# Forward convolution spread over more TensorE work: later transposes, eight residues for three more slices, and a drain one block later

## The chip, the cores and the metric

The kernel runs on one core of a Trainium2 chip. A core has TensorE (PE, matrix products into the accumulator memory PSUM), VectorE (DVE), ScalarE (ACT), GpSimd (POOL) and SyncE (SP), which share an on-chip memory (SBUF)[...]. The metric is the device time of one execution in microseconds (us). Before the change it is 1932.07 us, the median of three runs (1931.62 to 1939.0). The profile shown is of one execution with a span of 1928.7 us.

## The reference

The program computes a layer and its gradients. With S = 2048 rows, D = 1024 columns and F = 3584 hidden columns:

```
xn  = layernorm(q)                             # rows of 1024
ks  = causal 4-tap convolution of k over rows, one filter per column
kv  = ks * v
y   = causal convolution of kv with ssm_k over all 2048 rows (by FFT), per column
y   = y + kv * ssm_D
s   = xn * y
b   = ((xn @ w_gate) * (xn @ w_up)) @ w_down   # gate and up product, h, down product
out = q + s * silu(b)
outputs: out and the gradients to q, k, v, shift_k, ssm_k, ssm_D, w_gate, w_up, w_down
```

All inputs and outputs are bf16. The change touches the forward part alone: the layer norm, the gate and up product, the convolution y, and the beginning of the down product.

## The kernel before, in words

**Rows and slices.** The 2048 rows are 16 row blocks of 128. The F columns are 14 slabs of 256. The D columns of the convolution are eight slices of 128 (`ds`).

**Layer norm (`layer_norm`).** It works on chunks of rows: row blocks 0, 1, 2-3, 4-7, 8-11, 12-15. For each row block it normalises x on VectorE (for two of four blocks a part on ScalarE), turns the block with eight 128x128 transposes on TensorE into a PSUM tile `tr`, and copies that to `XNT`, alternately on ScalarE and VectorE. The norm of a chunk is recorded ahead of the products of the chunk before it.

**Gate and up product (`gu_unit`).** A unit is one slab by up to four row blocks. For each row block, eight matmuls of 512 columns go into `psg`, ScalarE copies the result to `gut`, and `tick()` is called. After a unit `multiply` makes h on VectorE (`hN`, 128x1024 in bf16, 60 such multiplies in all); five ticks later `turn` transposes it on TensorE and ScalarE copies it to `hT`, which is stored to `HTd`. `gut` is stored to `GUd`, h to `Hd`.

**Forward convolution (`conv_forward`).** It is a Python generator which records VectorE, ScalarE and TensorE instructions in small pieces and yields a weight for each. `tick` calls `pump`, which runs the generator until its summed weights reach the share of the total that the count of ticks gives; `NT` is the number of ticks that the total is spread over. So the convolution is interleaved with the products by this planned share[...]. For each slice, two spectra are made: matmuls with tables of sines and cosines into `psF`, ScalarE copies to `SP` (two buffers), sums on VectorE into `W`, then `KX` or `HX`. The spectra are multiplied (`product`), and the inverse begins with sums on VectorE and ends with matmuls into `psY` (`tail`), which ScalarE copies to `yf`, stored to `YFd`.

**Two forms of the inverse.** `inv_dft` with `inv_rows` folds the 16 residue segments with few VectorE sums and does 32 matmuls of 256 columns a slice. `inv8` with `inv8_rows` goes one level further on VectorE and does 16 matmuls. `INV8` lists the slices with the second form; before the change these are 2 and 5. `F_TOTAL` adds its weight.

**Down product (`bm_mm`, `bm_first`, the loop over `bp`).** Row block b of `h @ w_down` takes 28 times two matmuls of 512 columns into a PSUM tile `psbm`. Blocks 0 and 1 are done together (`bm_first`, with ticks of 0.74), in the two buffers of `ps_bm`. Then `drain()` records what is left of the convolution, the convolution's memory is released, and the gates of blocks 0 and 1 are recorded. The loop over `bp` from 1 to 7 does the blocks 2*bp and 2*bp+1. Block 2 is in a buffer of its own (`ps_bx`), block 3 uses the first buffer of `ps_bm` again, and so needs block 0's result copied away. The h columns of a pair come from `load_ht`; pairs from the second on alternate between two buffers, `mh0` and `mh1`.

**Gates (`gate`).** For a row block, four tiles are loaded by SyncE (`x_t`, `do_t`, `xn_t`, `yf_t`, two buffers each; `yf_t` reads what the convolution stored in `YFd`). ScalarE copies `psbm` to `bm` and makes two sigmoids, VectorE makes eleven products and sums of 128x1024 (the first are named `so`, `dgg`, `gg`), GpSimd stores four results (`dbm` goes to `DBMd`). After every four blocks a transposing load of `DBMd` is queued on SyncE.

The rest of the program is the backward part, whose code is unchanged.

Of the kernel before, what the change touches and what calls it, by code (L numbers as in the profile page):

```python
# [13 lines left out]
BF16 = mybir.dt.bfloat16  # L14
# [5 lines left out]
def build_kernel(  # L20
# [11 lines left out]
    nc = tc.nc  # L32
    P = 128
# [31 lines left out]
    def st(out, in_):  # L65
        ins = nc.gpsimd.dma_start(out=out, in_=in_)  # L66
        if PINQ[0]:
            tc.keep_in_program_order(ins)
        return ins
# [17 lines left out]
    def pool(name, bufs=1, side=None, space=None):  # L87
        kw = dict(name=name, bufs=bufs, reuse_waits="tile")
        if side:
            kw["side"] = side  # L90
        if space is not None:
            kw["space"] = space
        return tc.alloc_tile_pool(**kw)
# [455 lines left out]
            ld(x4[:, 0:n, :], xq[:, c, r0:r0 + n, :])  # L549

    tr_ln, act_copy = [None], [None]

    def layer_norm(b0, n, x4):
        def small(name, dt=F32):
            return lns.tile([P, 4], dt, name=name)[:, 0:n]
        mv = lns.tile([P, 4, 2], F32, name="mv")[:, 0:n, :]
        for i in range(n):
            bst = lns.tile([P, 2, 6], F32, name="bst")
            for hh in range(2):
                V.bn_stats(out=bst[:, hh, :], in_=x4[:, i, hh * 512:(hh + 1) * 512])  # L560
            V.bn_aggr(out=mv[:, i, :], in_=bst[:])
        var_b = small("var_b", BF16)
        V.tensor_copy(var_b, mv[:, :, 1])
        vpe = small("vpe", BF16)
        V.tensor_scalar(vpe, var_b, EPS, None, op0=ADD)
        r0_ = small("r0_")
        with tc.issue_after(act_copy[0].ins) if act_copy[0] is not None else nullcontext():
            root = nc.scalar.activation(r0_, vpe, ACT.Sqrt)
        mean_b = small("mean_b", BF16)
        V.tensor_copy(mean_b, mv[:, :, 0])  # L570
        rr0 = small("rr0")
        V.reciprocal(rr0, r0_)
        mean_f = small("mean_f")
        V.tensor_scalar(mean_f, mean_b, -1.0, None, op0=MUL)
        q0 = small("q0")
        tt(q0, vpe, rr0, MUL)
        r1 = small("r1")
        tt(r1, r0_, q0, ADD)
        sq_b = small("sq_b", BF16)
        V.tensor_scalar(sq_b, r1, 0.5, None, op0=MUL)  # L580
        V.reciprocal(RSTD[:, b0:b0 + n], sq_b)
        for i in range(n):
            b = b0 + i
            q, qi = divmod(b, 4)
            if n == 4 and i < 2:
                nc.scalar.activation(x4[:, i, :], x4[:, i, :], ACT.Identity, bias=mean_f[:, i:i + 1])
            else:
                V.tensor_scalar(x4[:, i, :], x4[:, i, :], mean_f[:, i:i + 1], None, op0=ADD)
            last = V.tensor_scalar(x4[:, i, :], x4[:, i, :], RSTD[:, b:b + 1], None, op0=MUL)
            if b < 2:  # L590
                for hh in range(2):
                    ps = ps_st.tile([P, 4, P], BF16, name="tr")
                    for dc in range(4):
                        d0 = (4 * hh + dc) * P
                        tr_ln[0] = nc.tensor.transpose(ps[:, dc, :], x4[:, i, d0:d0 + P], ident[:])
                    act_copy[0] = nc.scalar.copy(out=XNT[0][:, 4 * hh:4 * hh + 4, b * P:b * P + P], in_=ps[:])
                if b == 0:
                    with tc.issue_after(tr_ln[0].ins):
                        keep_busy(10)
                continue  # L600
            ps = ps_st.tile([P, DC, P], BF16, name="tr")
            for dc in range(DC):
                tr_ln[0] = nc.tensor.transpose(ps[:, dc, :], x4[:, i, dc * P:(dc + 1) * P], ident[:])
            if i % 2 == 0:
                act_copy[0] = nc.scalar.copy(out=XNT[q][:, :, qi * P:(qi + 1) * P], in_=ps[:])
            else:
                V.tensor_copy(XNT[q][:, :, qi * P:(qi + 1) * P], ps[:])
        c, r0 = divmod(b0, 8)
        return last, root, st(xnn[:, c, r0:r0 + n, :], x4[:, 0:n, :])

    nop = lambda: None
    nop1 = lambda c: None
# [6 lines left out]
    def flush(age=0):  # L619

        for e in later:
            e[0] += 1
        while later and later[0][0] >= age:
            later.pop(0)[1]()
# [5 lines left out]
    def gu_unit(sl, b0, n, w, tick):  # L630

        if n == 4:
            turn_of[0] += 1
            if turn_of[0] % 3 == 0 and sl < NSL - 2:
                gut = U[5][:, 2048:4096].rearrange("p (a i f) -> p a i f", a=2, i=4)
            else:
                gut = fg.tile([P, 2, 4, SLW], BF16, name="gut")
            hN = fg.tile([P, 2, 4, P], BF16, name="hN", bufs=3)
        else:
            gut = lnp.tile([P, 2, 2, SLW], BF16, name="gut_s", bufs=6)  # L640
            hN = lnp.tile([P, 2, 2, P], BF16, name="hN_s", bufs=6)
        for i in range(n):
            q, qi = divmod(b0 + i, 4)
            ps = ps_gu.tile([P, 512], F32, name="psg")
            for dc in range(DC):
                gu_mm[0] = nc.tensor.matmul(ps[:], XNT[q][:, dc, qi * P:(qi + 1) * P],  # L646
                                            w[:, dc].rearrange("p a f -> p (a f)"), start=(dc == 0), stop=(dc == DC - 1))
            nc.scalar.copy(out=gut[:, :, i], in_=ps[:].rearrange("p (a f) -> p a f", a=2))  # L648
            flush(5)
            hn[0]()  # L650
            hn[0] = nop
            tick()
        sta(GUd[sl, b0 // 8][:, :, b0 % 8:b0 % 8 + n], gut[:, :, 0:n])

        def multiply():
            with tc.issue_after(last.ins) if b0 + n <= 4 and chunk[0] <= 2 else nullcontext():
                by_half = lambda t: t.rearrange("p i (a f) -> p a i f", a=2)
                tt(hN[:, :, 0:n], by_half(gut[:, 0, 0:n]), by_half(gut[:, 1, 0:n]), MUL)
            st(Hd[sl][:, :, b0:b0 + n, :], hN[:, :, 0:n])
            defer(turn)  # L660
        hn[0] = multiply

        def store(hT):
            fr, so = sl % 12 * SLW, b0 % 8 * P
            ld(HTd[b0 // 8][sl // 12][fr:fr + SLW, so:so + n * P].rearrange("(a f) s -> f a s", f=P),
               hT[:, :, 0:n].rearrange("f a i s -> f a (i s)"))

        def turn():
            hT = fg.tile([P, 2, 4, P], BF16, name="hT") if chunk[0] > 5 else lnp.tile([P, 2, 4, P], BF16, name="hT_s", bufs=5)
            ps = ps_tr.tile([P, 2, 4, P], BF16, name="tr")  # L670
            for a in range(2):
                for i in range(n):
                    nc.tensor.transpose(ps[:, a, i, :], hN[:, a, i, :], ident[:])
            nc.scalar.copy(out=hT[:, :, 0:n], in_=ps[:, :, 0:n])
            store(hT)

    h_out = []
    EIGHT = ((0, 0), (0, 1), (7, 0), (7, 1))
    INV8 = (2, 5)
    SHIFT_W = 8 * 2.3  # L680

    conv_state = {"forward": True}
# [227 lines left out]
    ps_cv = pool("ps_cv", 2, space=PSUM)  # L910
    pump, drain = make_pump(conv, F_TOTAL)
    cnt = [-5]
    NT = 24 * 8.0 + 14

    def tick(by=1):
        cnt[0] += by
        if cnt[0] == -4:
            pump((SHIFT_W + 4.05) / F_TOTAL)
        if cnt[0] >= -2:
            pump((SHIFT_W + (F_TOTAL - SHIFT_W) * (cnt[0] + 5) / (NT + 2)) / F_TOTAL)  # L920

# [331 lines left out]
        ht1 = load_ht(1)  # L1253
    ht2 = load_ht(2)
    bm_first(range(4, NF))
    drain()
    PIN[0] = False
    mh.append(pool("mh1", 1, side="right"))
    mi = pool("mi", 2, side="right")
    mt = pool("mt", 1, side="right")  # L1260
    mo = pool("mo", 2, side="right")
    for i in range(2):
        gate(i, pss[i])
    for bp in range(1, 8):
        ht, ht_ld = load_ht(bp) if bp > 2 else (ht1, ht2)[bp - 1]
        if bp in (3, 5, 7):
            q = (bp - 3) // 2
            with tc.issue_after(ht_ld.ins):
                nc.sync.dma_start_transpose(out=DBMT[q], in_=DBMd[512 * q:512 * q + 512, :])
        if bp == 6:  # L1270
            with tc.issue_after(ht_ld.ins):
                wdt = load_wdt(0)
                gu_in(0)
        for i in range(2):
            ps = (ps_bx if (2 * bp + i) % 3 == 2 else ps_bm).tile([P, D], F32, name="psbm")
            for fc in range(NF):
                bm_mm(ps, ht, i, fc)
                if fc == 18:
                    flush()
            gate(2 * bp + i, ps)  # L1280
    for p_ in (ps_bx, ps_tr, ps_y, ps_bm, mo, mt, mi, mh[1], mh[0]):
        p_.release()
# [346 lines left out]
```

## Time and profile before

| | us |
|---|---|
| time, median of three runs | 1932.07 |
| span of the profiled execution | 1928.7 |
| PE busy | 1907.8 |
| VectorE busy | 1542.7 |
| ScalarE busy | 638.8 |
| PE waits on a row-block transpose for VectorE's normalised rows, four times | 2.4 |
| PE starts the block products of the down product | 519.62 |
| VectorE ends the forward convolution | 528.1 |
| last `psY` matmuls of the forward convolution start | 549.21 |

A line of the timeline gives the start and the length of a run of like instructions, the engine, the line of the code, the operation, the output and inputs by the program's names, the shapes, the count, and in brackets how long the engine was idle before it and what ended this. In the slices (40 of them, 48.2 us each) a digit is the busy share in tenths. An answer on waiting gives the engine that waited, what it waited for, the sum in us, how often, and the longest. PE's end times are modelled and overlap with the next start, so the starts are used to count PE's work.

### The profile page before, as it was taken

The numbers are of one execution on the slowest core, as the hardware profiler recorded it, in microseconds if no ns is written. First come the engines' busy times: TensorE is split into PE (matmuls) and PEld (weight loads), VectorE is DVE, ScalarE is ACT, GpSimd is POOL, SyncE is SP. The second block draws the span as 40 slices with busy tenths as digits, with TensorE's granted clock in tenths as the row PEclk, the third lists the DMA queues.
The fourth block names the chain that finished last, engine by engine and source line by source line (L and its number), as shares of the span: only waits on it lengthen the run. The fifth ranks groups of instructions, "written<-read, shape, count | busy, mean of one in ns | idle before, by whom it ended". The sixth has DMA issues, their size and how long they took to land.

```text
span 1928.7 us, 27377 instructions
## 1 busy us (share of the span) xinstructions
PE 1907.8 (99%) x10860; PEld 1032.3 (54%) x10994; DVE 1542.7 (80%) x1720; ACT 638.8 (33%) x942; POOL 328.7 (17%) x461
## 2 busy tenths in 40 slices
PE   8999999999999999999999999999999999999999
PEld 5555555555444457665666666664444444444444
DVE  9999999999937556888799999999996403488873
ACT  5854555556323233343222222222222102011122
POOL 4121211201112210000122131021111101011111
PEclk9999999999999999999999999999999999999999
DMA  8876866758879997666788788575787999799973
GB/s 294 267 243 229 256 216 219 248 185 290 294 227 310 285 313 260 208 203 218 250 247 257 250 244 264 199 273 178 222 255 173 157 209 214 167 188 188 192 207 117
DMA packets 451360, 444.43 MB, mean 230 GB/s; under 512 B 268800, under 2 KB 371612, under 8 KB 436768
## 3 DMA queue, kind: packets, MB, share of 16 engines
q1 hardware_dynamic: 394848, 243.36, 47.8%
q0 software_dynamic: 40064, 169.95, 27.5%
q10 hardware_dynamic: 16320, 29.36, 4.2%
q8 instruction: 86, 1.41, 0.3%
q14 instruction: 42, 0.34, 0.1%
HBM read 194.00 MB, written 185.64 MB: 197 GB/s over the span
## 4 chain that ended last, share of the span: by engine, by line
PE 84%; DVE 11%; issue 2%; ACT 1%; DMA 1%; SPq 0%; ACTq 0%; DVEq 0%
PE psb L1337 20%; PE psx L1467 20%; PE psb L1320 10%; PE psbm L967 10%; PE psb L1415 9%; PE psg L646 9%; DVE W L213 3%; DVE HX L213 2%; DVE KX L213 2%; PE psF L235 2%; DVE U L213 1%; DVE m L213 1%; PE psY L438 1%; DVE hN L213 1%; PE psY L1114 1%
## 5 line engine op out<-in xcount | busy, mean ns | idle before, releaser
L646 PE MATMUL psg<-wslab,U 128*128 128x512 bf16 x1735 | 400.5, 379 | 5.9 <-ACT gut L648 1.7
L1337 PE MATMUL psb<-U,U 128*128 128x512 bf16 x1792 | 397.1, 379 | 0.0
L1467 PE MATMUL psx<-U,dgut 128*128 128x512 bf16 x1505 | 331.1, 379 | 1.6
L1467 PEld LDWEIGHTS <-dgut 128*128 128x128 bf16 x1792 | 175.3, 98 | 211.5
L1337 PEld LDWEIGHTS <-U 128*128 128x128 bf16 x1792 | 175.2, 98 | 198.0
L646 PEld LDWEIGHTS <-U 128*128 128x128 bf16 x1792 | 172.5, 98 | 188.9 <-issue 3.5
L1320 PE MATMUL psb<-wdt,U 128*128 128x256 bf16 x1792 | 205.6, 273 | 0.0
L1320 PEld LDWEIGHTS <-U 128*128 128x128 bf16 x1792 | 175.2, 98 | 29.3
L1415 PE MATMUL psb<-U,U 128*128 128x512 bf16 x797 | 175.9, 380 | 0.9
L1342 ACT CAST wb<-psb 128x512 bf16<-128x512 f32 x112 | 65.5, 585 | 315.5 <-PE psb L1337 307.7
L213 DVE TENSOR_TENSOR W<-W 128x1024 f32<-128x1024 f32 (+1 forms) x168 | 165.4, 1001 | 3.6
L967 PE MATMUL psbm<-U,ht 128*128 128x512 bf16 x658 | 145.0, 379 | 0.7
L1415 PEld LDWEIGHTS <-U 128*128 128x128 bf16 x896 | 87.4, 98 | 104.6
L648 ACT CAST gut<-psg 128x512 bf16<-128x512 f32 x156 | 91.0, 587 | 129.4 <-PE psg L646 121.1
L1499 ACT ACTIVATE dx_t<-dxn 128x1024 bf16<-128x1024 f32 x15 | 15.9, 1057 | 324.8 <-DVE dxn L213 320.9
L967 PEld LDWEIGHTS <-ht 128*128 128x128 bf16 x672 | 65.6, 98 | 78.6
L213 DVE TENSOR_TENSOR U<-U,dht 128x2048 bf16<-128x2048 bf16 x56 | 68.3, 1221 | 45.9 <-ACT dht L1322 45.8
L1322 ACT CAST dht<-psb 128x512 bf16<-128x512 f32 x112 | 65.6, 586 | 116.4 <-PE psb L1320 116.4
L1166 DVE SCALAR_TENSOR_TENSOR dkp<-dkT,kT 128x1024 bf16<-128x1024 bf16 (+2 forms) x64 | 78.3, 1224 | 30.7 <-DMA dkT<-DKSHd 28.9
L213 DVE TENSOR_TENSOR dxn<-psx,dxna_t 128x1024 f32<-128x1024 f32 x15 | 18.3, 1222 | 87.9 <-PE psx L1467 83.9
L66 POOL DMA_DIRECT2D Hd<-hN x54 | 36.9, 684 | 263.3 <-DVE hN L213 261.0
L1446 ACT CAST wbs<-psb 128x512 bf16<-128x512 f32 x51 | 29.8, 585 | 145.1 <-PE psb L1415 131.2
(256 smaller groups left out, 2464.5 us busy)
## 6 DMA issues: line engine op xcount, KB each, us to landing
U<-GUd SPq DMA_DIRECT2D x28, 1024.0 KB, 7.6
DGd<-U SPq DMA_DIRECT2D x28, 1024.0 KB, 5.8
GUd<-gut ACTq DMA_DIRECT2D x39, 512.0 KB, 6.3
out_dram<-wb SPq DMA_DIRECT2D x112, 128.0 KB, 4.2
U<-Hd SPq DMA_DIRECT2D x14, 1024.0 KB, 6.5
Hd<-hN POOLq DMA_DIRECT2D x54, 256.0 KB, 5.0
HTd<-hT SPq DMA_DIRECT2D x52, 256.0 KB, 3.9
ht<-HTd SPq DMA_DIRECT2D x6, 1536.0 KB, 13.2
```

The lines of the kernel that those rows point to most:

```text
L213: pinned(V.tensor_tensor(o, a, b, op))
L235: mm = nc.tensor.matmul(ps[:, k].rearrange("p (c d) -> p c d", c=2), T[:, r, k, :], xr[:, r], start=(n == 0), stop=(n == len(rs) - 1 and ( ...
L646: gu_mm[0] = nc.tensor.matmul(ps[:], XNT[q][:, dc, qi * P:(qi + 1) * P], w[:, dc].rearrange("p a f -> p (a f)"), start=(dc == 0), stop=(dc ...
L648: nc.scalar.copy(out=gut[:, :, i], in_=ps[:].rearrange("p (a f) -> p a f", a=2))
L967: mm = nc.tensor.matmul(ps[:, dh * 512:(dh + 1) * 512], ht(fc)[:, i * P:(i + 1) * P], WD[fc // 4][:, fc % 4, dh * 512:(dh + 1) * 512], sta ...
L1166: ins = V.scalar_tensor_tensor(prod[:].rearrange("p r d -> p (r d)")[:, lo:H], dkT[:, 0, lo:H], 1.0, kT[:, 0, 13 + m + lo:13 + m + H], op0 ...
L1320: nc.tensor.matmul(ps[:, x * SLW:(x + 1) * SLW], DBMT[2 * hf + g][:, dc, (b % 4) * P:(b % 4 + 1) * P], wdt[:, dc, :], start=(dc == 0), sto ...
L1322: nc.scalar.copy(out=dht[:, 2 * e:2 * e + 2].rearrange("p b f -> p (b f)"), in_=ps[:])
L1337: nc.tensor.matmul(ps[:], XN[b // 4][:, b % 4, dc * P:(dc + 1) * P], dgus[b // 8][:, :, b % 8], start=(b == 0), stop=(b == NB - 1))
L1342: nc.scalar.copy(out=wb[:, dc % 2].rearrange("p a f -> p (a f)"), in_=ps[:])
L1415: nc.tensor.matmul(ps, h[:, f, b, :], DBM[b // 4][:, b % 4, dh * 512:(dh + 1) * 512], start=(b == 0), stop=(b == NB - 1))
L1467: nc.tensor.matmul(ps[:, dh * 512:(dh + 1) * 512], t[n][:, f, i * P:(i + 1) * P], WGU[n][:, f, dh * 512:(dh + 1) * 512], start=(n == 0 and ...
```

## The change

There are three edits to the forward part. They are meant to fill TensorE's waits in the beginning, to take matmuls off it, and to give the convolution a longer stretch of products to lie beside.

1. The transposes of row blocks 8 to 15 are not recorded in `layer_norm`. They are kept in `turn_rows`, and `turn_late()` records them after the first row block of the next gate and up unit.
2. Slices 1, 4 and 6 use `inv8` too.
3. The convolution is spread over four more ticks (`NT`), 14 ticks of 0.37 are added in block 2 of the down product, and the drain, the release of memory, the new pools and the gates of blocks 0 and 1 come behind block 2's matmuls.

```diff
+    turn_rows = []
...
+            if b0 >= 8:
+                turn_rows.append((x4[:, i, :], q, qi))
+                continue
             ps = ps_st.tile([P, DC, P], BF16, name="tr")
...
+    def turn_late():
+        for i, (x, q, qi) in enumerate(turn_rows):
+            ps = ps_st.tile([P, DC, P], BF16, name="tr")
+            for dc in range(DC):
+                tr_ln[0] = nc.tensor.transpose(ps[:, dc, :], x[:, dc * P:(dc + 1) * P], ident[:])
+            if i % 2 == 0:
+                act_copy[0] = nc.scalar.copy(out=XNT[q][:, :, qi * P:(qi + 1) * P], in_=ps[:])
+            else:
+                V.tensor_copy(XNT[q][:, :, qi * P:(qi + 1) * P], ps[:])
+        turn_rows.clear()
...
             flush(5)
+            if i == 0:
+                turn_late()
             hn[0]()
...
-    INV8 = (2, 5)
+    INV8 = (1, 2, 4, 5, 6)
...
-    NT = 24 * 8.0 + 14
+    NT = 24 * 8.0 + 18
...
     bm_first(range(4, NF))
-    drain()
-    PIN[0] = False
-    mh.append(pool("mh1", 1, side="right"))
-    mi = pool("mi", 2, side="right")
-    mt = pool("mt", 1, side="right")
-    mo = pool("mo", 2, side="right")
-    for i in range(2):
-        gate(i, pss[i])
     for bp in range(1, 8):
...
                 if fc == 18:
                     flush()
+                if 2 * bp + i == 2 and fc % 2 == 1:
+                    tick(0.37)
+            if 2 * bp + i == 2:
+                drain()
+                PIN[0] = False
+                mh.append(pool("mh1", 1, side="right"))
+                mi = pool("mi", 2, side="right")
+                mt = pool("mt", 1, side="right")
+                mo = pool("mo", 2, side="right")
+                for j in range(2):
+                    gate(j, pss[j])
             gate(2 * bp + i, ps)
```

## The prediction

> **What bounds the kernel now.** I read the page's slices first, then the busy table of three stretches, then who waits for whom, then single lines of the timeline around each edit.
>
> ```profile
> PE   8999999999999999999999999999999999999999
> DVE  9999999999937556888799999999996403488873
> ```
> ```profile
> 64.00:520.00 456.00, 448.74 (x2767) 252.65 (x2817) 447.11 (x405) 259.24 (x366) 76.42 (x109) 1.00 0.72 241
> 520.00:560.00 40.00, 39.72 (x208) 20.07 (x212) 9.60 (x9) 9.98 (x12) 1.83 (x2) 1.00 0.62 180
> 560.00:722.00 162.00, 161.22 (x769) 75.50 (x783) 104.03 (x165) 47.39 (x47) 37.98 (x60) 1.00 1.04 307
> ```
> The columns of the second fence are the stretch, its length, then PE, PEld, DVE, ACT and POOL busy, clock, DMA share and GB/s. PE looks like the bound everywhere. But in 64 to 520 us, the gate and up product with the forward convolution, VectorE is as full as PE (447 of 456 us). It rests after 528 us, and from 560 us the DMA engines are full (1.04).
>
> Which of two full engines sets the pace is told by waits. From the answers on waiting (whole program, then 64 to 560 us):
>
> ```profile
> ACT SP L257 <- DVE W L213: 4.2, 6, 1.4
> PE psF L235 <- ACT SP L257: 1.4, 5, 0.3
> DVE hN L213 <- ACT U L648: 4.3, 1, 4.3
> ```
> ```profile
> 427.87 1.93 ACT L257 COPY SP<-psF 128x1024 f32<-128x1024 f32 x2 [0.43 <-DVE W L213]
> ```
> ```profile
> 428.93 1.95 PE L235 MATMUL psF<-hx,TF 128*128 128x256 bf16 x16 [0.34 <-ACT SP L257]
> ```
> PE waits for ScalarE's spectrum copy, which waits for VectorE to have read the older copy. The waits are short, but they come back in slice after slice: in six of the eight slices the first copies of the second transform start 0.1 to 0.6 us after VectorE's read. VectorE itself waits three times: 4.28 us at 135.41, 0.43 at 496.11, 0.61 at 520.44; its other gaps add to 4.1 us in 105 pieces. So VectorE leads this stage, and PE keeps up by a small margin.
>
> [...] the 128x2048 f32 `W<-KX` takes 2,292 ns. So f32 operations of 512 columns, which the edit adds, can't be cheap: the trace has them at 686 ns. [...] the trace has 49 matmuls in 10.74 us, 216 ns, and I use that. [...] waits on PE are up to 0.16 us longer than printed (379 ns shown, 216 ns spacing). [...]
>
> **Part 1, late transposes.** Rows 8 to 15: the same 64 transposes and 8 evictions, behind eight matmuls instead of ahead of them. They remove two PE waits, 0.71 us at 37.32 and 0.64 at 48.26, 1.4 to 1.7 us with the hidden part. In 20 to 60 us VectorE is busy 39.1 of 40 us, and the order of the new kernel has the same VectorE work ahead of every h multiply up to 88 us. I take 0 for the end (bounds 0 and -1.7).
>
> **Part 2, eight residues in slices 1, 4, 6.** PE: 16 fewer 128x256 matmuls a slice; eight take 0.87 us (543.14 to 544.01), so 1.74 us a slice, 5.2 us in all. VectorE: `inv8` has the same two 2.29 us reads and, for four 1.22 us operations, four others of the same size, plus ten of 512 columns (four HX sums, two W, four scaled sums). Two such take 1.29 us, overlapped about 0.64 each: 6.4 us a slice, 19.2 us in all. VectorE leads, so this counts, except what fits in its rest or moves past the stage.
>
> **Part 3, convolution into the third block.** With the weaker ticks (NT 18) the last multiply (the 60th `hN`) has more convolution behind it. In the order before there remain HX, W, HX (2.36+2.29+2.36 = 7.0 us). In the new order also KX, m, two KX, W, HX, W, HX: 1.22+1.22+2.36+2.29+2.36+2.29+2.36 = 14.1 us. So 7.1 of the 19.2 us leave the stage and 12.1 stay. The order also puts 11.4 us more VectorE work ahead of the multiply at 135.41, which closes its 4.28 us hole; a slower VectorE doesn't meet the 0.43 and 0.61. The last multiply starts at 520.44+12.1-4.28-1.04 = 527.2, ends at 527.9, and its transposes follow at 527.95. Before:
>
> ```profile
> 524.78 0.61 PE L673 MATMUL tr<-ident,hN 128*128 128x128 bf16 x8
> 543.14 1.04 PE L449 MATMUL psY<-HX,TI 128*128 128x256 bf16 x8
> 549.21 1.04 PE L449 MATMUL psY<-HX,TI 128*128 128x256 bf16 x8
> 550.09 22.61 PE L967 MATMUL psbm<-U,U 128*128 128x512 bf16 x102
> ```
> At 524.78, same place in PE's order: **+3.2 us**, PE's 5.2 us spent in waiting. If all 4.1 us of small gaps went too, -0.9; if the hole stays open, +7.5.
>
> VectorE's tail then ends at about 527.9+14 = 542; the first `psY` of slice 7, 144 block matmuls after the block start instead of 104, comes at about 555. No wait there.
>
> **What the drain's move queues up.** In the new order four block matmuls (0.86 us) stand between the last `psY` and block 3, whose first matmul waits for ScalarE's `bm` of block 0. That came at 550.77 to 551.78, 2.57 us after the last `psY` started (549.21). PE gets there after 0.87+0.86 = 1.73 us: **+0.9 us**. Block 2 used to hide this.
>
> The gates of blocks 0 to 2 begin 44 matmuls later in PE's order, 9.5 us, 8.6 relative to PE after that wait. Their chain was not held by PE: the last YFd store (551.2, 6.6 us to land), `yf_t`, then gates 0 to 4 back to back with two DMA waits. Behind them in SyncE's queue stands the h load of the fifth block pair, which block 8 needs:
>
> ```profile
> 593.24 5.16 SPq L1269 DMA_TRANSPOSE U<-DBMd  x1
> 598.49 0.68 SPq L61 DMA_DIRECT2D do_t<-in_grad_out_dram  x1
> 601.18 0.60 SPq L61 DMA_DIRECT2D ht<-HTd  x1
> ```
> ```profile
> DMA to landing us min/median/max: 15.5/15.5/15.5
> ```
> ```profile
> 621.12 1.01 ACT L1198 CAST bm<-psbm 128x1024 bf16<-128x1024 f32 x1 [9.04 <-PE psbm L967]
> ```
> The second fence is of the load at 601.18 alone: landed 616.7. The DBMd transpose ahead of it starts when gate 3's store has landed (593.17). Block 8 starts at 620.9, as block 7's copy at 621.12 shows: a margin of 4.2 us. Shifted by 8.6, the load is 4.4 us late: **+4.4 us**, from 0 (with less traffic such a load takes 10 us, the median) to 7 (still more beside it). Later loads of this kind are issued at PE's release, with 14 us in hand.
>
> **Sum.** 3.2+0.9+4.4 = +8.5: 1932.1+8.5 = 1940.6 us. After block 8 the order is unchanged and PE hardly waits, so nothing gives it back.
>
> **Rivals.**
> - PE is the true bound. -5.2-1.6+0.9 = -5.9: 1926.2 us, faster. For it: PE 99%, printed waits tiny. Against: the copies tied to VectorE in six slices.
> - VectorE sets the pace, but the load arrives in time since its traffic thins out: +3.2+0.9 = +4.1, 1936.2 us. For it: other such loads take 10 us; against: the same transpose and gate loads stand around it.
> - VectorE loses more: the hole doesn't close (+4.3) and the load is 6 to 7 us late: about +15, 1947 us. For it: the DMA share of 1.04. Against: the new order has work ready for the hole.
>
> **How the numbers follow.** Forecast 0.45, PE bound 0.12, load in time 0.28, loses more 0.15. Leaving out PE bound and the upper half of the last, the range runs from 1930 (all gaps closed, load in time, some PE gain) to 1947. 0.5% is 9.7 us: slower means over 1941.7. That takes the last rival (0.15) and some 0.4 of the forecast (0.18): 0.33. Faster needs under 1922.4, which no case gives: 0.04. The rest, 0.63, is within.
>
> **What would show it.** Step 2 right: 19 us more VectorE work before the gates, with no gap at 135 us. Step 3: the last h transposes near 528 us, and new PE waits on `hN` or `SP` between 430 and 528. Then a wait of PE on `bm` of about 0.9 us at block 3, and one on `ht<-HTd` at block 8 of 2 to 6 us. Wrong if block products start before 517 us (PE was the bound), if the h load lands before block 7 ends, or if a wait appears after 720 us.

## The result and the profile after

The changed kernel takes 1944.14 us, the median of four runs (1942.38 to 1945.96), beside 1931.84 us for the kernel before (median of four). The ratio is 1.0055, with a 95% interval of 1.003 to 1.008: it is slower, and the ratio lies just over the half per cent that was to tell it from no change, though its interval reaches to both sides of that. The forecast of 1940.6 us was 3.5 us too low; the range of 1930 to 1947 holds the time. All runs of this case are in the same, fast state, and the ratios here and below are formed from all of them and not from two medians, so a ratio can differ from that of the medians. The profiled execution has a span of 1942.3 us, 13.6 us over the one before.

The page's slices after, for the two engines shown before:

```profile
PE   9999999999999999999999999999999999999999
DVE  9999999999938654888899899999997403487884
```

The two pictures are nearly the same: the slices don't show where 13.6 us went. The busy table of the three stretches does a little more (columns as in the prediction):

```profile
64.00:520.00 456.00, 441.67 (x2702) 247.01 (x2751) 451.12 (x424) 256.29 (x363) 74.89 (x108) 1.00 0.70 231
520.00:560.00 40.00, 36.97 (x184) 17.35 (x186) 22.25 (x18) 4.47 (x6) 1.68 (x3) 1.00 0.79 248
560.00:722.00 162.00, 159.11 (x750) 73.91 (x764) 98.13 (x156) 50.52 (x51) 36.57 (x57) 1.00 1.02 285
```

VectorE is busy 451 of 456 us in the first stretch (447 before) while PE's work there fell from 448.7 to 441.7. In the second PE lost 2.75 us of its 39.7, in the third 2.1 us. The answer on PE's waits names all the places:

```profile
PE psF L235 <- ACT SP L257: 8.4, 4, 3.1
PE tr L1237 <- DVE dbm L213: 2.9, 1, 2.9
PE psbm L984 <- DMA U<-in_B_w_down_dram: 2.5, 1, 2.5
PE psg L661 <- ACT gut L663: 2.1, 2, 1.9
PE psbm L984 <- DMA ht<-HTd: 1.4, 1, 1.4
...
PE tr L619 <- DVE U L590: 0.9, 2, 0.7
...
PE psbm L984 <- ACT bm L1215: 0.7, 1, 0.7
```

The wait on `SP` was 1.4 us before; the waits on `dbm`, on the `w_down` tile (`WD[6]`), on `ht` and on `bm` did not exist. The timeline of PE puts them in time, and the last transposes of h beside them:

```profile
528.35 0.62 PE L690 MATMUL tr<-ident,hN 128*128 128x128 bf16 x8 [0.32 <-DVE hN L213]
547.66 10.48 PE L984 MATMUL psbm<-U,U 128*128 128x512 bf16 x47 [2.50 <-DMA U<-in_B_w_down_dram]
567.75 12.25 PE L984 MATMUL psbm<-U,U 128*128 128x512 bf16 x55 [0.73 <-ACT bm L1215]
629.72 2.55 PE L984 MATMUL psbm<-U,ht 128*128 128x512 bf16 x11 [1.37 <-DMA ht<-HTd]
726.49 0.62 PE L1237 MATMUL tr<-ident,dbm 128*128 128x128 bf16 x8 [2.90 <-DVE dbm L213]
726.95 5.74 PE L984 MATMUL psbm<-U,ht 128*128 128x512 bf16 x17
```

The last two lines had no wait and full speed before:

```profile
714.58 0.61 PE L1220 MATMUL tr<-ident,dbm 128*128 128x128 bf16 x8
715.03 4.05 PE L967 MATMUL psbm<-U,ht 128*128 128x512 bf16 x17
```

How late PE stands at the same instruction of both traces turns these waits into a sum. The first block product starts at 522.89 us, 3.27 later than before. By ScalarE's copy of each block's result (`bm`), blocks 6 and 7 stand at +7.31, blocks 8 to 14 at +8.85 (one copy at +9.13), and the end of block 15 at +13.61; from there to the end nothing changes. So the 13.6 us are

| step | us | of it |
|---|---|---|
| gate and up stage | 3.27 | waits on `SP`, 8.4 in all (1.4 before); one has a halved clock behind it |
| blocks 0 to 5 | 4.04 | `WD[6]` 2.5, `bm` 0.73, each with 0.16 of hidden part (the prediction's 379 ns against 216), 0.5 of small ones |
| block 8 | 1.54 | `ht` 1.37 and the hidden part |
| block 15 | 4.76 | `dbm` 2.90 and the hidden part, and 1.7 of a halved clock |

The halved clock is seen in the last line of each of the two fences above: the same 17 recorded matmuls take 5.74 us where they took 4.05 before. The busy table of three short stretches shows the granted clock (third number from the end):

```profile
204.80:208.20 3.40, 3.20 (x16) 2.28 (x16) 3.40 (x4) 2.07 (x3) 0.00 (x0) 0.50 0.00 0
318.30:321.70 3.40, 2.83 (x21) 2.04 (x21) 3.40 (x4) 3.04 (x4) 0.00 (x0) 1.00 0.00 0
727.10:730.50 3.40, 3.40 (x10) 1.21 (x8) 1.96 (x3) 1.01 (x1) 0.71 (x2) 0.50 1.00 400
```

Beside PE waits of 3.12 us (up to 205.00) and 2.90 us (up to 726.49) it runs at 0.50 for 3.41 us, from 204.82 and from 727.06; after one of 2.69 us (up to 318.87) it stays at 1.00.

### The profile page after: what moved, and what is told of

It is laid out like the page before. It is cut to its first block, busy times and chain, and to the rows that moved or that the text cites. A ratio compares the mean times of both kernels' runs of the same rounds, so it can differ in the third digit from the quotient of the medians.

```text
span 1942.3 us, 27309 instructions
## 1 busy us (share of the span) xinstructions
PE 1907.1 (98%) x10813; PEld 1028.7 (53%) x10946; DVE 1561.6 (80%) x1750; ACT 638.2 (33%) x942; POOL 328.7 (17%) x461
## 4 chain that ended last, share of the span: by engine, by line
PE 62%; issue 0%; ACT 0%; DVE 0%; ACTq 0%
PE psb L1357 20%; PE psx L1487 20%; PE psb L1340 10%; PE psb L1435 9%; PE psY L1131 1%; PE psY L438 1%; PE psx L1435 1%; PE psF L235 1%; PE psbm L984 0%; PE psY L1435 0%; ACT B L295 0%; DVE dbm L213 0%; PE tr L1237 0%; ACT wbs L1582 0%; ACT wb L1362 0%
## 5 line engine op out<-in xcount | busy, mean ns | idle before, releaser
L213 DVE TENSOR_TENSOR W<-W 128x1024 f32<-128x1024 f32 (+1 forms) x186 | 184.0, 1005 | 3.9
L1466 ACT CAST wbs<-psb 128x512 bf16<-128x512 f32 x51 | 29.8, 585 | 145.3 <-PE psb L1435 134.4
```

The lines of the kernel that those rows point to most:

```text
L213: pinned(V.tensor_tensor(o, a, b, op))
```

## Experiments

Runs 1 to 3 take the change apart and run 4 goes the other way; all four begin with the kernel before. "First" is the start of the first block product, "span" that of the profiled execution, both as us over the kernel before; the ratio is to the runs of before on the same chip.

| run | kernel | median, us | ratio (95%) | first | span |
|---|---|---|---|---|---|
| 1 | late transposes alone | 1931.24 | 1.0001 (0.9992 to 1.0009) | -0.1 | -0.1 |
| 2 | five slices alone | 1943.32 | 1.0064 (1.005 to 1.0078) | +11.8 | +11.8 |
| 3 | moved drain alone | 1949.55 | 1.0099 (1.0082 to 1.0115) | -0.65 | +19.1 |
| 4 | before with no slice of eight residues | 1930.71 | 0.9995 (0.9987 to 1.0004) | +0.4 | +0.4 |
| 5 | changed, turns a block later | 1943.81 | 1.006 (1.0047 to 1.0072) | +3.9 | +12.4 |
| 6 | run 3, turns a block later | 1940.46 | 1.0053 (1.0033 to 1.0073) | +0.2 | +5.2 |
| 7 | changed, plain `DBMd` loads | 1939.58 | 1.0039 (1.0026 to 1.0052) | +2.9 | +8.1 |
| 8 | mix of three slices | 1954.6 | 1.0106 (1.0071 to 1.0142) | +3.75 | +14.9 |
| 9 | changed, `DBMd` loads later | 1963.92 | 1.0174 (1.015 to 1.0199) | +3.8 | +46.1 |
| 10 | run 8, third load later | 1955.16 | 1.0113 (1.0087 to 1.014) | +3.0 | +22.1 |
| 11 | before with three slices | 1933.07 | 1.0009 (1.0001 to 1.0017) | +5.6 | +5.6 |
| 12 | before with one slice | 1930.41 | 0.9992 (0.9986 to 0.9998) | -0.3 | -0.3 |

A profile is one execution, and not always one near the median. Those of runs 6 and 8 (1935.69 and 1945.37 us) lie 5 and 9 us below their medians; that of run 9 (1976.61 us) is the slowest of six, 13 us above.

**Run 1: part 1 alone.** The edit is the first part of the diff, on the kernel before.

> Part 1 alone on the kernel before. VectorE leads the stage: 0 (between -0.5 and +0.3 us), and only one of the two early PE waits (0.71 at 37.3, 0.64 at 48.3) goes, as in the changed kernel, where 0.71 and 0.17 stayed. PE is the bound: the removed wait shows at the end, -0.6 to -1.6 us.

The ratio is 1.0001: nothing. In the trace, as in that of the changed kernel, the wait of 0.71 us near 37.5 is still there, now of the late transposes themselves (`tr L619` in the waits above), and the one of 0.64 became 0.17. So the edit removed half a microsecond of PE's waits in a stretch where VectorE is full, and it doesn't show at the end.

**Run 2: part 2 alone.**

```diff
-    INV8 = (2, 5)
+    INV8 = (1, 2, 4, 5, 6)
```

> Part 2 alone: three more slices with eight residues, the drain at its old place. PE 5.2 us less work, VectorE 19 us more. VectorE leads: nothing moves behind the last hN, so the last hN and the first block products come 8 to 14 us later than before (hole of 4.28 us partly closed), and most of it stays to the end: +6 to +14 us. PE is the bound: about -5 us.

PE has 5 us less to do, and the kernel is 12.2 us slower: PE isn't the bound of this stage. All of it stands at the first block product (+11.8), and nothing is added later. The stage's row of the busy table, then PE's waits from 64 to 560 us, then a line of VectorE's timeline, all of run 2:

```profile
64.00:520.00 456.00, 436.68 (x2655) 243.84 (x2705) 451.64 (x424) 254.50 (x357) 75.45 (x107) 0.99 0.69 229
```
```profile
PE psF L235 <- ACT SP L257: 12.6, 5, 4.3
PE psF L235 <- DVE kv L213: 1.7, 1, 1.7
PE tr L673 <- DVE hN L213: 1.6, 1, 1.6
```
```profile
535.08 0.69 DVE L213 TENSOR_TENSOR hN<-gut 128x1024 bf16<-128x1024 bf16 x1
```

VectorE has no gap over 0.25 us from 60 to 540 us. The last line is the last h multiply. The prediction's own working, without the 7.1 us that part 3 moves behind it, puts it at 520.44 + 19.2 - 4.28 - 1.04 = 534.3 us; it started at 535.08. None of the later waits appear here: the `w_down` tile landed at 548.37 us, but PE, 11.8 us late itself, hadn't come to it by then.

**Run 3: part 3 alone.** `NT`, the ticks in block 2, and the drain, pools and gates behind block 2, with `INV8 = (2, 5)`.

> Part 3 alone with the old two slices of eight residues: convolution thinner ahead of the last hN. VectorE leads: block products start 2 to 6 us earlier than before (PE cannot gain more than its own waits), but the costs behind stay as in the changed kernel: WD load late 2.7, bm of block 0 0.9, h load at block 8 1.5, and 4.8 at block 15 (2.9 us wait with 1.7 us of halved clock), so in all +4 to +10 us. If those late waits come from VectorE's extra work instead of the moved drain and gates: they are absent and the time is -1 to -5 us. PE is the bound: +1.

This is the costliest part: +18.5 us, more than the whole change, and more than any branch of the expectation allowed. The waits on `dbm`, `ht` and `bm` are there with the two old slices, so VectorE's extra work isn't what makes them. The stage is 0.65 us shorter, where 2 to 6 had been expected, so everything is lost in the blocks. PE's waits of the whole program, the longest first:

```profile
PE tr L1220 <- DVE dbm L213: 12.2, 2, 8.2
PE psbm L967 <- DMA ht<-HTd: 2.5, 1, 2.5
```

The two waits on `dbm` are 8.19 us in block 13 and 4.00 in block 15, and 10.2 us of half clock go with them. Of these 2.8 lie within the first wait (the half clock runs from 698.02 to 704.84, the wait ends at 700.80), so 7.4 us at half speed cost 3.7. 12.2 + 3.7 + 2.5 (`ht`) + 0.7 (`bm`), with 0.16 of hidden part each, is 19.8, and -0.65 leads to +19.1. The 5.1 us in the expectation of run 6 counts the 2.8 too. SyncE's queue shows what the gates waited for. In this view the length is how long SyncE was held by the issue:

```profile
698.73 0.46 SPq L61 DMA_DIRECT2D x_t<-in_A_q_dram  x1
699.30 16.53 SPq L1261 DMA_TRANSPOSE U<-DBMd  x1
715.94 0.54 SPq L61 DMA_DIRECT2D do_t<-in_grad_out_dram  x1
716.92 0.33 SPq L61 DMA_DIRECT2D xn_t<-XNd  x1
717.35 0.40 SPq L61 DMA_DIRECT2D yf_t<-YFd  x1
```

The third transposing load of `DBMd` held the queue for 16.5 us and landed 24.0 us after its start, and the gate's four loads behind it landed from 724.8 to 726.8. In the trace of the kernel before this load took 15.2 us, but that is the longest of the six traces with the drain at its old place: they run from 6.3 us (run 11) to 15.2, and none has a wait on `dbm`.

**Run 4: the other direction.** `INV8 = ()` in the kernel before.

> Kernel before with no slice of eight residues: PE +3.5 us of matmuls, VectorE -12.8 us. VectorE leads: PE's waits of the stage vanish, the added matmuls lie in them, -2 to +1 us. PE is the bound: +3.5 us.

-0.4 us, so neither a bound on PE (+3.5) nor one on VectorE (which has 12.8 us less, by the prices of part 2) is seen. PE's waits on `SP` fall from 1.4 to 0.7 us, and PE is busy 452.2 of 456 us in the stage (448.7 before), so the added matmuls fill its small gaps. At two slices the two engines are in balance: work added to VectorE costs, work taken off it brings nothing, since PE is right behind.

**Runs 5 and 6: is it the wait in block 15?** `turn`, the transposes of a gate's `dbm` on PE, one row block later; run 5 in the changed kernel, run 6 in that of run 3.

```diff
                 if fc == 18:
-                    flush()
+                    flush(2)
```

> The changed kernel with the turns of gates 12 to 14 recorded one row block later (flush of age 2 in the loop). If the wait of 2.90 us at 726.49 and the halved clock behind it (1.7 us) cost what the trace shows: -4.8 us against the changed kernel, +8.8 against the kernel before, about 1940.6. If the gates' transfers are late anyway and PE only waits for them further on: 0 against the changed kernel.

> The moved drain alone (two slices of eight residues, as the run before with the drain alone), with the turns of gates 12 to 14 one row block later. If the 8.19 and 4.00 us of PE's waits and the 5.1 us of halved clock were its cost: +19.1 - 17.3 = about +2 us against the kernel before, from 0.7 (bm) + 2.5 (h load) - 0.65 (earlier block products). If late transfers hold PE further on: still +10 or more.

Run 5: the wait and its halved clock are gone from the trace, and the time isn't: 1943.81 us, as before the edit. PE's waits from 520 us on are now

```profile
PE psbm L984 <- DMA ht<-HTd: 2.8, 1, 2.8
PE psbm L984 <- DMA U<-in_B_w_down_dram: 2.3, 1, 2.3
PE psbm L984 <- ACT bm L1215: 0.7, 1, 0.7
```

with the clock halved behind the 2.84 us on `ht` (the 31 matmuls recorded there take 8.77 us, 283 ns each beside the prediction's 216): PE loses 4.7 us at block 8 instead of 1.5. Also, the third transposing load took 8.2 us from issue to landing here and 22.1 in the changed kernel's trace. SyncE's issue of it, in run 5 and then in the changed kernel:

```profile
695.66 5.05 SPq L1278 DMA_TRANSPOSE U<-DBMd  x1
```
```profile
694.75 12.27 SPq L1278 DMA_TRANSPOSE U<-DBMd  x1
```

The edit moves transposes on PE that come after the issue (from 698.4 us on in the changed kernel), which hardly explains that. And this shorter load, not the edit, took the wait away: gate 14's `dbm` was ready at 725.16, before PE reached the place in block 15 where the unedited order turns it (726.56). It rather seems that the length of such a load changes from one execution to the next, as the spread of the runs suggests (1939.11 to 1947.75 us in run 5), and a trace holds one of them. The 4.76 us of block 15 are right for the execution profiled; that the median has them is not shown. Run 6's trace has no wait after 630 us and stands at +5.2, where +2 was expected; about half of the difference is a halved clock (1.7 us) behind its `ht` wait of 2.3 us (mean clock 0.96 from 600 to 640 us). Here too the `dbm` of gates 12 and 14 were ready before PE came to their old places in blocks 13 and 15 (693.37 against about 694.8, one block ahead of 706.85, and 717.99 against 719.38), so the trace doesn't test the edit either. The eleven runs spread from 1934.99 to 1954.36 us, and their median is +8.9, 9.1 us under run 3's, with intervals that don't meet. That speaks for the `dbm` waits having carried a large share of run 3's cost, but not all of it; no trace shows it.

**Run 7: plain loads in place of the transposing ones.** The edit leaves out the turning of `DBMd`, so two of the weight gradients aren't those of the reference.

```diff
-                nc.sync.dma_start_transpose(out=DBMT[q], in_=DBMd[512 * q:512 * q + 512, :])
+                ld(DBMT[q].rearrange("p a (b d) -> p (a b) d", b=4)[:, :, :], DBMd[512 * q:512 * q + 512, :].rearrange("(p a) (b d) -> p (a b) d", a=4, d=128))
```

> The changed kernel with the three transposing loads of DBMd as plain loads of the same bytes; it leaves out the turning, so the gradients made from them are other numbers. If the transposing form is what keeps the loads behind it waiting (15 to 24 us each): the h load for block 8 and the loads of gate 14 come in time, -1.5 and -4.8, so -6.3 us against the changed kernel. If the bytes or the late start of the gates do it: 0 to -2.

The third load lands 5.9 us after its issue, no wait is left after 630 us, the one on `ht` is 0.94 us, and the span is 5.5 us shorter than the changed kernel's; the medians differ by 4.6 us, though the intervals overlap (to 1.0052, from 1.003). The four runs lie within 4.2 us. The 4.6 us lie between the two branches of the expectation. Four runs against four suggest that the same bytes in a plain load disturb the block stage less, so that the form of this load is part of the cost.

**Runs 8 to 10: better places for these loads.** Run 8 puts together what seemed good: slices 2, 4, 5, the moved drain, the turns later, and the first transposing load behind the h load of block 8. Runs 9 and 10 record the third behind gate 15's loads too, run 9 in the changed kernel.

```diff
-        if bp in (3, 5, 7):
+        if bp in (4, 5):
...
+    nc.sync.dma_start_transpose(out=DBMT[2], in_=DBMd[1024:1536, :])
```

(Run 8 has `(4, 5, 7)` and no added line.)

> Moved drain and late transposes with three slices of eight residues (2, 4, 5), the turns one row block later, and the first transposing load of DBMd behind the h load of block 8. The moved drain takes 7.1 us of VectorE work out of the stage and a third slice puts 6.4 back, so block products start as in the run with the drain alone less PE's 1.7: -1 to -2.4. Behind it only the bm wait (0.7 to 0.9) and perhaps the WD load (0 to 2.7) are left: -1.5 to +2 us against the kernel before. If the gates' late start costs PE in itself: +5 or more.

> The changed kernel with two of the three transposing loads of DBMd moved in SyncE's queue: the first behind the h load of block 8, the third behind the loads of gate 15. If what stands behind such a load in the queue is late because of it: the waits at block 8 (1.4 us) and block 15 (2.9 us with 1.7 of halved clock) go, -6.3 against the changed kernel, about 1938. If the gates' transfers are late for their sheer amount: 0 to -2, or a new wait for the third load itself after 740 us.

> The mix of three slices of before (moved drain, late transposes, slices 2, 4, 5, turns later), with the third transposing load of DBMd behind gate 15's loads as well. If the order of the queue is what made the mix slow behind block 13: no waits after 720 us, and only bm (0.7) and a WD load (0 to 2.7) stand against PE's 1.7 us less work: -2 to +2 us against the kernel before. If the late gates cost PE in themselves: +5 or more.

All three missed the time that was hoped for by some 20 us and more; runs 8 and 10 fall under their other branch (+5 or more), though not for its reason alone. Run 8 did lose the wait on `ht` (0.2 us) and that on `WD[6]`. But ScalarE waited 5.57 us for an earlier store of `hT` at 476.6, so PE waited 4.8 us for `gut` there, and the third load took 26.4 us, after which gate 15's `dbm` held PE for 3.8 us. In run 9 the first load no longer stood before the h load of block 8, but before that of block 10. SyncE's queue in run 9, then PE's waits in the whole program:

```profile
624.96 23.28 SPq L1278 DMA_TRANSPOSE U<-DBMd  x1
...
650.51 0.41 SPq L61 DMA_DIRECT2D ht<-HTd  x1
```
```profile
PE psbm L984 <- DMA ht<-HTd: 20.0, 2, 10.9
PE tr L1237 <- DVE dbm L213: 8.2, 1, 8.2
```

The load held the queue 23.3 us and landed after 29.8; the h load behind it landed at 663.61, and PE waited 10.9 us for it, and 9.06 for the next. The third load, recorded last, was still issued ahead of gate 14's loads in both kernels (728.27 and 738.12 in run 9, 701.39 and 714.07 in run 10): the program's order isn't the recorded one, so this part of the edit didn't do what it was made for, and its question wasn't answered. In run 10 the worst wait was for `A<-DYd` at 770.67 (7.99 us), in flight beside yet another transposing load (`wdt`, 26.5 us).

**Runs 11 and 12: how many slices?** The kernel before with `INV8 = (2, 4, 5)` and with `(5,)`.

> Kernel before with slices 2, 4, 5 of eight residues, drain at its old place: VectorE +6.4 us, PE -1.7. VectorE leads only where its holes are used up: 6.4 less the 4.28 hole and 1.04 of small waits, about +1 (0 to +4). PE is the bound: -1.7. Proportional to the five slices' +11.8: +3.9.

> Kernel before with slice 5 alone of eight residues: VectorE -6.4 us, PE +1.7. If the two engines are in balance at two slices: -1 to +0.5 us, since PE's waits take up its added work, as in the run with none. If PE alone were the bound: +1.7.

With the runs of none, two and five, as ratios: 0.9995, 0.9992, 1, 1.0009, 1.0064 for 0, 1, 2, 3 and 5 slices. It is flat up to two and then rises: 1.7 us for the third, about 10.6 more for the fourth and fifth. Proportion to the five slices' cost would have put three at +3.9. The trace of run 11 is above its own median: +5.6 us, in it two stretches of half clock behind waits of 2.2 us (mean clock 0.99 from 64 to 520 us, 1.00 in the kernel before). One slice, 1.5 us (0.4 to 2.7) under the kernel before, is the only version whose interval lies below both kernels, and a little better than was expected (-1 to +0.5).

## Why the prediction was nearly right

**What bounds the stage: right.** VectorE leads it once work is added. Run 2 shows it: less PE work, more time, and all of it ahead of the first block product. The rival with PE as the bound (1926.2 us) falls with the same run. "By a small margin" was right too: runs 4 and 12 take VectorE work away and nothing, or 1.5 us, comes back.

**Part 1, 0: right** (run 1). That it would remove both PE waits was wrong: the late transposes still meet VectorE late, by 0.71 and 0.17 us.

**Part 2, sizes: right.** VectorE's busy time rose by 18.9 us (19.2 predicted). PE has 48 matmuls fewer by the working, and 47 fewer records on the page.

**Part 3, the stage: right.** The last multiply was put at 527.2 and started at 527.61, its transposes at 527.95 and started at 528.35; +3.2 at the first block product, measured 3.27. The 4.28 us hole closed: VectorE's longest gap from 60 to 560 us is 0.48. The new waits on `SP` came earlier than the prediction looked for them: 3.12 us at 205.00 and 2.69 at 318.87, and only 1.63 between 430 and 528. The halved clock near 205 us, not foreseen, is inside the 3.27. In the trace of run 5, with a second such stretch at 318, the stage is only 0.6 us longer: while VectorE leads, PE's loss mostly lies in a wait that PE would have anyway. Beside runs 2 and 3 one sees what parts 2 and 3 are to each other: five slices cost 11.8 in the stage, and the move behind block 2 takes 8.5 of it away again.

**`bm` of block 0, +0.9: right** (0.73 and the hidden 0.16).

**The h load, +4.4: right in kind, too large.** It was issued at 614.98, 13.8 us later than before, and landed at 629.67, 14.7 us after the issue (15.5 before). PE reached block 8 later too, by 7.31 us and not by 4.1, so that the wait was 1.37. The landing itself was put at 629.4 by the working (616.7 + 8.6 + 4.1). The term that was mis-sized is how late PE itself is by then, which is the next step.

**Failed: "What the drain's move queues up".** The step listed the drain, the gates, and one load behind them, and took the rest as having time in hand: "After block 8 the order is unchanged and PE hardly waits, so nothing gives it back." Two things stand against it.

- `WD[6]`, +2.66. This tile's memory held h, and SyncE issues its load when the last two stores of h have landed (in the changed kernel the last landed 4.1 us after 537.68, and the load was issued at 541.89). Those stores, then the load, before and in the changed kernel (x2 are two stores with a gap between them):

```profile
524.76 2.07 SPq L61 DMA_DIRECT2D HTd<-hT  x2
531.22 0.37 SPq L61 DMA_DIRECT2D U<-in_B_w_down_dram  x1
```
```profile
528.99 2.23 SPq L61 DMA_DIRECT2D ht<-HTd  x1
531.31 6.73 SPq L61 DMA_DIRECT2D HTd<-hT  x2
541.89 0.37 SPq L61 DMA_DIRECT2D U<-in_B_w_down_dram  x1
```
```profile
536.64 1.01 ACT L691 COPY hT<-tr 128x1024 bf16<-128x1024 bf16 x1 [8.64 <-DMA HTd<-hT]
```

  PE turned the last h only 3.6 us later than before, but its store went out 11.2 us later (537.68): ScalarE's copy waited 8.64 us for an earlier store of `hT`. That store had been issued at 524.72 and landed at 536.56, behind an h load of the third block pair, issued at 517.76 (502.01 before), and a `w_down` load. The h load goes into memory that VectorE's convolution frees, 15.7 us later than before. So the load of `WD[6]` landed at 547.62 (536.86 before): 10.8 us later, where PE was only 3.3 us later and had had 5.0 in hand (it came to the tile at 545.16, so at about 541.9 before). The prediction followed PE's path from the last h to the blocks, and not the second path from the same h, through stores and buffers. Neither part alone shows this wait: in run 2 PE itself is late, and in run 3 the load lands at 539.86, some 1.4 us before PE comes.

- Block 15, +4.76 in this trace. The late gates don't end with block 8: the transposing load of every four gates moves with them, and the loads of the next gates stand behind it. The third such load started 2.3 us later than before against PE, and took 22.1 us instead of 15.2, so most of the lateness is its own length. VectorE shows gate 14 waiting for them:

```profile
720.68 0.69 DVE L213 TENSOR_TENSOR so<-xn_t,yf_t 128x1024 bf16<-128x1024 bf16 x1 [9.85 <-DMA yf_t<-YFd]
```

  From there the products run back to back to `dbm` (725.75), and PE, whose transposes of it stand in the middle of block 15, waits. The prediction had named this as a sign of being wrong ("a wait appears after 720 us"), and it appeared.

In the trace these two misses make +7.4 and the smaller h load -2.9; with +0.6 of small things that is the 5.1 us between the sum of +8.5 and the measured 13.6. By the medians the gap is 3.8 us (12.3 to 8.5). That it isn't wider is in part luck: the h load's term was 2.9 us too large, and hid so much of what was left out.

**What stays open.** What makes one such transposing load take 6.5 us from issue to landing in one execution (run 2's third) and 29.8 in another (run 9's first) isn't settled. Run 7 suggests that its form matters, run 9 that its place does. Where the third one stands, from 680 to 720 us, the changed kernel's DMA engines are fuller and move less: 242 GB/s at a share of 1.14, beside 302 at 0.99 in the kernel before. Nor is it shown why the blocks lose 19.7 us with the drain moved alone and 10.3 in the changed kernel; the second and third transposing loads took 18.8 and 24.0 us in the one trace, 11.7 and 22.1 in the other. The third load behind gate 14's loads, the order that would tell most, wasn't reached.

## What to carry to other kernels

When work is moved past the end of a stage, follow every queue and every buffer that it feeds, to the last load behind it, and write down how much time each has in hand; the path of the busiest engine is only one of them. Two edits that look like partners should be timed alone too: here each costs more than 10 us, and together they cost no more than the cheaper one. Where two engines are in balance, trading work between them has a flat optimum: none to two slices here, and about 0.1% to be had.

## What the hardware showed that was not expected

- **PE's clock after short waits.** In the changed kernel the clock was 0.50 for 3.41 us beside waits of 3.12 and 2.90 us, as shown with the result, and 1.00 after one of 2.50 us (at 547.66). In run 6 one of 2.3 us, on `ht`, came with a halved clock too (0.96 as the mean from 600 to 640 us, which is 3.2 us at half). The same wait of 2.69 us, at 318.63 in run 5 and at 318.87 in the changed kernel, halved the clock in the first

```profile
318.30:321.70 3.40, 3.07 (x15) 2.14 (x15) 3.40 (x4) 2.21 (x3) 0.00 (x0) 0.51 0.00 0
```

  and not in the second (1.00 in the fence with the result). The 16 matmuls that end the wait took 3.42 us in the first and 1.95 in the second. So of four waits of 2.3 to 2.7 us two came with a halved clock and two without; what tells them apart isn't shown, and no run changed such a wait on purpose.
- **Issuing isn't always cheap.** With the transposing loads SyncE was held 5.05 us of the 8.2 from issue to landing in run 5, 12.27 of 22.1 in the changed kernel, 16.53 of 24.0 in run 3 and 23.28 of 29.8 in run 9, and its later loads with it: in run 3 the next one was issued at 715.94, behind the 16.53 us that began at 699.30. Long holds aren't theirs alone: a gate's plain load of 256 KB held SyncE for 11.11 us at 601.88 in the kernel before, right behind the h load.
- **Spread.** With the drain moved, runs of one kernel spread by 10 to 23 us in five of these kernels (runs 3, 6, 8, 9 and 10) and by 4 to 9 in the other three (the changed kernel, runs 5 and 7), beside 2.2 us in thirteen runs of run 4. The kernel before spread by 9.5 us in 35 runs, by 4.2 without its slowest. One trace of such a kernel doesn't stand for its median.
